# Chunked attention and a gated MLP on one core: v tiles used twice, keys put in place by two copies, a new order of the first blocks

## The chip, the core and the metric

The kernel runs on one core of a Trainium2 chip. The metric is the device time of one execution in microseconds. The kernel before takes 733.04 us, the median of 3 runs (732.32 to 733.74). One further execution was recorded by the profiler; every row shown here is from it.

The core's engines each work through a list of their own and wait for one another by semaphores: TensorE (PE in the rows, its weight loads PEld) multiplies matrices, VectorE (DVE), ScalarE (ACT) and GpSimd (POOL) work elementwise, SyncE (SP) issues most DMAs. SBUF is the working memory of 128 partitions, PSUM the one that TensorE writes.

## What is computed

Attention over 4 batches, 8 heads, 768 positions of 64 numbers, in chunks of 32 queries. A chunk sees 8 memory rows, 16 positions to its left, its own 32 and 8 to its right. The result goes through a gated MLP with RMS norm:

```python
for c in range(nc):                                   # 24 chunks of 32
    k_ctx = k[:, :, max(0, 32*c - 16):min(S, 32*c + 40)]      # v_ctx alike
    k_full = np.concatenate([mem_k, k_ctx], axis=2)           # v_full alike
    a = softmax(q_c @ k_full.T / 8)
    out[:, :, 32*c:32*c + 32] = a @ v_full
x = out as (3072 tokens, 512)
xn = x / sqrt(mean(x * x) + 1e-6) * rms_g
return (silu(xn @ w_gate) * (xn @ w_val)) @ w_out     # 512 -> 1536 -> 512
```

## The kernel before

**Tiling.** Tokens are cut into 8 blocks of 384. A unit of attention is one pair of heads in one block, four units a block. Blocks 0 and 1 (units 0 to 7, the two halves of batch 0) are done first, beside the preparation of the weights; the other blocks' units are done later between the MLP's matmuls. Each weight is used as the sum of a high and a low part, so each product of the MLP is three passes (`PASS`): the group of twelve matmuls for one hidden group of 128 is `pg` (gate) or `pv` (up), the group of nine is `po` (output). The two parts are made in the kernel: a chunk of weights arrives by DMA, ScalarE makes two passes over it (`w_open`, lines 508 and 509), VectorE does bit operations (`w_clamp`, `w_sign`, `w_shift`), ScalarE rounds it (`w_high`), VectorE subtracts (`w_low`, line 532). Chunks come in threes, gate, up, output: the first three hold hidden group 0, the next three groups 1 and 2.

**An early unit.** q and k arrive with four positions in each partition. TensorE transposes them (`t` for q, `T` for k) into PSUM. `Q` copies q into a tile that holds the two heads on separate halves. `K`, `n`, `c` copy k into the tile `kw`, which has for each chunk a column group of 64: 8 memory keys, 16 left, 32 own, 8 right. `p` lets GpSimd write the memory columns of `kw`. `V` fills the unit's v tile `vw` with copies of the memory rows and of the column of ones (for the softmax's sum), and `w` loads the v rows into it, 56 rows for each pair of chunks. Then: scores `S`, maximum `M`, subtraction `a`, exponential `E`, transpose `P`, its two copies `C` and `m`, the product with v `O`, and `X`, `x`, `u`, which divide by the sum. `A`, `B`, `D` transpose a finished block and split it into `xh` and `xl`.

**What sets the order.** Up to the middle of the MLP of blocks 0 and 1, the order on each engine is that of a string of tokens, `ORDER`: a letter from the list above and a unit or step, and at the end, where there is one, the engine that copies (a ScalarE, d VectorE, g GpSimd). The rest is ordered by a planner. `Z` loads the next weight chunk, `J F f I H L` are the six steps over it, `g v h i j k l o` the MLP (up to `g5`, `SEQ` tells which block and group), `W` runs matmuls on zeros. SyncE issues DMAs in the string's order as well; an issue waits for the eighth issue before it to land.

In the listing and the rows lines have the numbers of the kernel before. `finish` writes the last block.

Of the kernel before, what the change touches and what calls it, by code (L numbers as in the profile page):

```python
# [18 lines left out]
NM = 8  # L19
# [28 lines left out]
U0 U1 U2 V1a U3 V2a V3d V0g Z p1 T0 Q0a p0 t1 n0d c0a p3 w0 K0a Q1a S0 p2 T1 M0 p4 w1 a0 t2 c1a  # L48
K1a n1d e0 T2 Q2a S1 E0 n2d K2d c2a Z J P0 M1 p5 w2 t3 C0a f m0a S2 a1 Q3a T3 p6 M2 E1 U4 a2 P1 w3
O0 n3d m1a F C1a K3d V4g c3a O1 E2 X0 I U5 S3 x0 V5g J X1 u0 U6 P2 x1 M3 p7 W8 C2a Z f m2a w5 a3  # L50
Ha O2 u1 E3 L V6g P3 X2 t4 F m3a U7 x2 C3a I T4 Q4a w6 u2 O3 K4d c4a N0 n4d V7g X3 S4 x3 w4 u3 t5
M4 Ha a4 T5 Q5a L T6 c5a n5d Y0 K5d Z K6d t6 w7 n6d c6a y0 E4 S5 Q6a P4 M5 r0 S6 z0 C4a m4a W4 a5
J M6 t7 E5 f T7 a6 Q7a F P5 n7d K7d m5a A0 c7a I C5a S7 B0a Ha A1 M7 W5 B1a D0 E6 a7 Z A2 J D1 A3
L O4 B2a f W9 X4 E7 D2 B3a x4 P6 F W6 C6a D3 m6a u4 O5 Z J I O6 X5 f P7 g0 Ha X6 x5 x6 u5 C7a m7a
u6 v0 h0 F N1 L Z I O7 J X7 i0 Ha x7 g1 j0 u7 k0a L Y1 l0 v1 y1 f Z h1 r1 z1 o0 J i1 F j1 A12 A11
I B12a A13 B11a g2 D12 k1a Ha l1 Z D11 B13a A10 L v2 B10a h2 D10 J i2 o1 D13 f j2 g3 J F f k2a l2
v3 I h3 i3 Z Ha o2 f j3 F g4 k3a L l3 I v4 h4 i4 J Z F g5 Ha f j4 I o3 L Ha v5 k4a F Z J l4 L h5
o4 i5 I g6 j5 Ha f k5a l5 v6 J Z L h6 f o5 i6 F j6 g7 F k6a l6 I J o6 f Z h7 v7 F Ha i7 I g8 j7 Ha
I k7a l7 Ha v8 Z L h8 i8 J o7 L j8 L g9 k8a l8 F Z J o8 f h9 f v9 F i9 I g10 J j9 Z f k9a Ha F v10
l9 I h10 i10 o9 Ha I Z j10 Ha L g11 k10a l10 J L o10 h11 F i11 Z J f v11 L f I F g12 Ha j11 I k11a  # L60
Z J l11 v12 f Ha F L h12 i12 o11 L j12 Z J I g13 f k12a F Ha I v13 L Ha l12 L h13 Z J o12 i13 f
j13 F g14 k13a I l13 Ha L Z J o13 f h14 F I v14 i14 Ha L g15 j14 Z J k14a f l14 F v15 h15 I i15 Ha
g16 j15 J L f F o14 I Ha L v16 k15a l15 h16 o15 i16 j16
# [4 lines left out]
def tile_kernel(ctx: ExitStack, tc: tile.TileContext, q, k, v, mem_k, mem_v,  # L68
# [49 lines left out]
    late_kv = {}  # L118
    KW, VW = (NC + 1) * KC, NJ * 2 * (D + 1)
# [54 lines left out]
    def stage_v(u, e="a"):  # L174
# [4 lines left out]
        d["v"] = vw = unit_tile(u, [P, NJ, 2, D + 1], "vw", NG)  # L179
# [73 lines left out]
    def stage_k0(u, e="d"):  # L253
        own = NM + LC
        k4 = split4(st[u]["tk"], HT + CH)
        copy(e, st[u]["kw"][:, :, own:own + CH].rearrange("p c (k r) -> p c k r", r=4), k4)

    def stage_l0(u, e="d"):
        z = units[u][1] + NC
        k4 = split4(st[u]["tk"], HT + CH)  # L260
        copy(e, st[u]["kw"][:, 1:z, NM:NM + LC].rearrange("p c (k r) -> p c k r", r=4), k4[:, 0:z - 1, (CH - LC) // 4:])

    def stage_c0(u, e="a"):
        a = units[u][1]
        k4 = split4(st[u]["tk"], HT + CH)
        copy(e, st[u]["kw"][:, a:NC, KC - RC:KC].rearrange("p c (k r) -> p c k r", r=4), k4[:, a + 1:NC + 1, 0:RC // 4])
# [345 lines left out]
    def finish(f, g, vv, po, blk):  # L612
# [10 lines left out]
        for i in range(NT):  # L623
# [168 lines left out]
    def tok_o(n):  # L792
# [9 lines left out]
        T=stage_kt, t=stage_qt, K=stage_k0, n=stage_l0, c=stage_c0, p=new_kw, Q=stage_q0,  # L802
# [126 lines left out]
```

## Time and profile before

| | |
|---|---|
| median of 3 timed runs | 733.04 us |
| profiled execution | 731.54 us |
| its span in the trace | 729.8 us |
| TensorE, VectorE, ScalarE, GpSimd busy | 715.1, 380.0, 287.8, 36.4 us |
| mean granted clock of TensorE | 0.995 of full |
| bytes moved | 50.20 MB |

The span is the time from the first to the last recorded instruction; the execution's own time is 1.7 us more. A row of the timeline has the start in us, the length in us, engine, line, operation, what is written and from what, the shape and the count; at its end in brackets the idle time before it and what ended that. A row of groups has busy us and the mean in ns of one, and behind the second bar the idle time before these instructions. In the chain of waits each piece is what the next piece waited for.

### The profile page before, as it was taken

To read this page: it belongs to the slowest core of one execution; us is meant where nothing else is said; L and a number is where in the kernel's file an instruction comes from. 1 tells how busy PE (TensorE), PEld (TensorE's weight loads), DVE (VectorE), ACT (ScalarE), POOL (GpSimd) and SP (SyncE) were. 2 spreads that over 40 slices of the span, in tenths; PEclk is the share of its full clock that TensorE was granted. 3 is DMA by queue.
4 is the path that set the end of the run, shared out by engine and by line. 5 is a ranking of instruction groups with operands and counts; after the bars stand their busy time and mean duration, and the time that the engine had idled before them with its cause. 6 is when DMAs were issued, how large, how long until landed. Compare 5 with 4: busy or idle time off the path is not lost.

```text
span 729.8 us, 13052 instructions
## 1 busy us (share of the span) xinstructions
PE 715.1 (98%) x5136; PEld 656.6 (90%) x5136; DVE 380.0 (52%) x725; ACT 287.8 (39%) x600; POOL 36.4 (5%) x143
## 2 busy tenths in 40 slices
PE   8889999999999999999999999999999999999997
PEld 7778999999989999899999999989998999999996
DVE  4888999865645443444535353445434543332222
ACT  4899676643452323422333232432234222341112
POOL 3300000001000000000000000000000000000000
PEclk8999999999999999999999999999999999999999
DMA  8994563414412320122212123021311210010001
GB/s 173 203 259 141 173 202 116 132 37 102 85 37 68 55 50 22 62 46 42 43 38 66 23 45 61 20 66 31 66 29 34 64 32 20 20 44 0 1 1 43
DMA packets 143173, 50.20 MB, mean 69 GB/s; under 512 B 126984, under 2 KB 134536, under 8 KB 143112
## 3 DMA queue, kind: packets, MB, share of 16 engines
q1 hardware_dynamic: 139832, 44.49, 26.6%
q10 hardware_dynamic: 3280, 4.88, 1.8%
q8 instruction: 40, 0.66, 0.4%
q14 instruction: 21, 0.17, 0.1%
HBM read 43.06 MB, written 6.29 MB: 68 GB/s over the span
## 4 chain that ended last, share of the span: by engine, by line
PE 92%; ACT 3%; DMA 3%; DVE 1%; issue 0%; POOL 0%; ACTq 0%; SPq 0%; POOLq 0%
PE pv L561 28%; PE po L599 28%; PE pg L561 27%; PE s L318 3%; PE o L368 3%; PE xT L440 1%; PE pT L348 1%; DMA ws<-in_moe_w_val_dram 1%; DMA memV<-in_mem_v_dram 1%; DMA vw<-in_v_dram 1%; ACT junk L398 0%; ACT ws L508 0%; ACT pt L227 0%; DMA kv<-in_v_dram 0%; ACT qb L227 0%
## 5 line engine op out<-in xcount | busy, mean ns | idle before, releaser
L561 PE MATMUL pv<-xh,wh_v 128*128 128x384 f32 x384 | 132.8, 346 | 0.0
L561 PE MATMUL pg<-xh,wh_g 128*128 128x384 f32 x384 | 129.7, 338 | 0.7 <-DVE t L572 0.7
L561 PE MATMUL pv<-xh,wl_v 128*128 128x384 f32 x384 | 129.5, 337 | 0.6 <-DVE wl_v L532 0.6
L561 PE MATMUL pg<-xh,wl_g 128*128 128x384 f32 x384 | 129.5, 337 | 0.0
L561 PE MATMUL pg<-xl,wh_g 128*128 128x384 f32 x384 | 129.3, 337 | 0.0
L561 PE MATMUL pv<-xl,wh_v 128*128 128x384 f32 x384 | 129.3, 337 | 0.0
L572 DVE SCALAR_TENSOR_TENSOR t<-t,pg 128x384 f32<-128x384 f32 x96 | 53.1, 553 | 138.6 <-ACT t L568 138.5
L227 ACT CAST hh<-t 128x384 fp32r<-128x384 f32 x95 | 48.7, 512 | 174.9 <-PE po L599 165.3
L599 PE MATMUL po<-wh_o,hh 128*128 128x512 f32 x285 | 113.8, 399 | 0.3
L599 PE MATMUL po<-wh_o,hl 128*128 128x512 f32 x285 | 113.1, 397 | 0.0
L599 PE MATMUL po<-wl_o,hh 128*128 128x512 f32 x285 | 112.1, 393 | 0.0
L584 DVE TENSOR_TENSOR hl<-t,hh 128x384 fp32r<-128x384 f32 x95 | 52.9, 557 | 100.7 <-ACT hh L227 95.7
L568 ACT ACTIVATE t<-pg 128x384 f32<-128x384 f32 x96 | 47.2, 492 | 135.9 <-PE pg L561 130.8
L575 DVE TENSOR_TENSOR t<-t,pv 128x384 f32<-128x384 f32 x95 | 52.5, 552 | 64.9 <-PE pv L561 64.4
L561 PEld LDWEIGHTS pg<-xh,wh_g 128*128 128x128 f32 x384 | 72.1, 188 | 4.4 <-DVE t L572 0.9
L561 PEld LDWEIGHTS pg<-xl,wh_g 128*128 128x128 f32 x384 | 72.1, 188 | 3.6
L561 PEld LDWEIGHTS pv<-xh,wh_v 128*128 128x128 f32 x384 | 72.1, 188 | 2.4
L561 PEld LDWEIGHTS pv<-xh,wl_v 128*128 128x128 f32 x384 | 72.2, 188 | 0.9 <-DVE wl_v L532 0.9
L561 PEld LDWEIGHTS pv<-xl,wh_v 128*128 128x128 f32 x384 | 72.2, 188 | 0.3
L561 PEld LDWEIGHTS pg<-xh,wl_g 128*128 128x128 f32 x384 | 72.1, 188 | 0.0
L599 PEld LDWEIGHTS po<-wh_o,hl 128*128 128x128 f32 x285 | 53.5, 188 | 14.1 <-DVE hl L584 1.8
L599 PEld LDWEIGHTS po<-wh_o,hh 128*128 128x128 f32 x285 | 53.5, 188 | 10.0 <-ACT hh L227 1.7
(112 smaller groups left out, 772.9 us busy)
## 6 DMA issues: line engine op xcount, KB each, us to landing
kn<-in_k_dram SPq DMA_DIRECT2D x96, 52.0 KB
qn<-in_q_dram SPq DMA_DIRECT2D x96, 48.0 KB
out_dram<-ob ACTq DMA_DIRECT2D x18, 256.0 KB
ws<-in_moe_w_gate_dram SPq DMA_DIRECT2D x4, 1024.0 KB
ws<-in_moe_w_val_dram SPq DMA_DIRECT2D x4, 1024.0 KB
ws<-in_moe_w_out_dram SPq DMA_DIRECT2D x4, 1024.0 KB
kv<-in_v_dram SPq DMA_DIRECT2D x48, 84.0 KB
kv<-in_v_dram SPq DMA_DIRECT2D x48, 70.0 KB
```

Of the source, the lines that this page charges most:

```text
L227: return nc.scalar.copy(out, in_)
L318: on_pe(nc.tensor.matmul(s[64 * par:64 * par + 64, o:o + KC], lhsT=qb[:, c].rearrange("p s q -> p (s q)"), rhs=kw[:, c], start=True, stop= ...
L348: on_pe(nc.tensor.transpose(out=t[:, i * P:(i + 1) * P], in_=pe[:, i * P:(i + 1) * P], identity=ident))
L368: on_pe(nc.tensor.matmul(o[64 * par:64 * par + 64, c0:c0 + D + 1], lhsT=pt[:, i, 2 * par + hh].rearrange("p c q -> p (c q)"), rhs=d["v"][: ...
L440: on_pe(nc.tensor.transpose(out=t[:, i * P:(i + 1) * P], in_=tiles[i][:, kt * P:(kt + 1) * P], identity=ident))
L561: on_pe(nc.tensor.matmul(ps[:, 0:HT], lhsT=weight(a, n, f, kt), rhs=xs[c][:, kt], start=cnt == 0, stop=cnt == 3 * NKT - 1))
L568: nc.scalar.activation(t, g, AF.Tanh, scale=0.5)
L572: nc.vector.scalar_tensor_tensor(out=t, in0=t, scalar=1.0, in1=g, op0=ALU.add, op1=ALU.mult)
L575: nc.vector.tensor_tensor(out=t, in0=t, in1=vv, op=ALU.mult)
L584: nc.vector.tensor_tensor(out=hl, in0=t, in1=hh.bitcast(F32), op=ALU.subtract)
L599: on_pe(nc.tensor.matmul(po[i], lhsT=h[a][:, i * P:(i + 1) * P], rhs=weight(c, "o", f), start=f == 0 and n == 0, stop=f == NF - 1 and n == 2))
```

## The change

The v tiles of units 4 to 7 are those of units 0 to 3, with their memory rows still in place; GpSimd clears the 32 last rows of the last chunk pair (behind the end of the sequence) and writes the column of ones of the other half. A unit's keys are put in place by two copies: `K` writes left, own and right columns of eleven chunks at once (616 columns, ScalarE), reading overlapping windows; `n` writes the columns of the chunk at the open end (40 or 48, VectorE). `c` is gone. The last half of the last rows has a tile of its own and is stored by ScalarE's queue. The string is written anew.

```diff
 ORDER = """
-U0 U1 U2 V1a U3 V2a V3d V0g Z p1 T0 Q0a p0 t1 n0d c0a p3 w0 K0a Q1a S0 p2 T1 M0 p4 w1 a0 t2 c1a
+U0 U1 U2 U3 V0d p1 V1d Z V2d V3d T0 Q0a p0 w2 t1 n0d K0a p3 p2 Q1d S0 w0 T1 M0 a0 t2 K1a n1d e0
...
     def stage_v(u, e="a"):
...
-        d["v"] = vw = unit_tile(u, [P, NJ, 2, D + 1], "vw", NG)
+        if NG <= u < NE:
+
+            d["v"] = vw = first_v[u - NG]
+            nc.gpsimd.memset(vw[96:P, NJ - 1, :, 0:D], 0.0)
+            nc.gpsimd.tensor_copy(out=vw[:, :, :, D], in_=ones[hf])
+            return
+        d["v"] = vw = first_v[u] = unit_tile(u, [P, NJ, 2, D + 1], "vw", NG)
...
     def stage_k0(u, e="d"):
-        own = NM + LC
-        k4 = split4(st[u]["tk"], HT + CH)
-        copy(e, st[u]["kw"][:, :, own:own + CH].rearrange("p c (k r) -> p c k r", r=4), k4)
+
+        t = st[u]["tk"]
+        n = (HT + CH) // 4
+        src = bass.AP(t.tensor, t.offset + (CH - LC) // 4, [t.ap[0], [CH // 4, NC - 1], [1, (KC - NM) // 4], [n, 4]])
+        copy(e, st[u]["kw"][:, 1:NC, NM:KC].rearrange("p c (k r) -> p c k r", r=4), src)
 
     def stage_l0(u, e="d"):
-        z = units[u][1] + NC
-        k4 = split4(st[u]["tk"], HT + CH)
-        copy(e, st[u]["kw"][:, 1:z, NM:NM + LC].rearrange("p c (k r) -> p c k r", r=4), k4[:, 0:z - 1, (CH - LC) // 4:])
-
-    def stage_c0(u, e="a"):
-        a = units[u][1]
-        k4 = split4(st[u]["tk"], HT + CH)
-        copy(e, st[u]["kw"][:, a:NC, KC - RC:KC].rearrange("p c (k r) -> p c k r", r=4), k4[:, a + 1:NC + 1, 0:RC // 4])
+
+        hf = units[u][1]
+        k4 = st[u]["tk"][:, 0:HT + CH].rearrange("p (r k) -> p k r", r=4)
+        a, z = ((NM, KC - RC) if hf else (NM + LC, KC))
+        k0 = (NC * CH - LC) // 4 if hf else 0
+        copy(e, st[u]["kw"][:, NC * hf, a:z].rearrange("p (k r) -> p k r", r=4), k4[:, k0:k0 + (z - a) // 4])
...
             nc.scalar.activation(o[:, a], po[i][:, a], AF.Copy, scale=0.5)
-            nc.vector.tensor_scalar(out=o[:, b], in0=po[i][:, b], scalar1=0.5, scalar2=None, op0=ALU.mult)
+            ob = p1.tile([P, HT], F32, name="ob", tag="t")[:, 0:DM // 2]
+            nc.vector.tensor_scalar(out=ob, in0=po[i][:, b], scalar1=0.5, scalar2=None, op0=ALU.mult)
             nc.sync.dma_start(out=out[rows, a], in_=o[:, a])
-            nc.sync.dma_start(out=out[rows, b], in_=o[:, b])
+            nc.scalar.dma_start(out=out[rows, b], in_=ob)
```

What this makes of the lists is shown at three places; numbers behind the names tell tiles apart. The first is SyncE's list, where the second set of weight chunks is loaded (gate 128x4x512, up, output) beside unit 7's q and k (`qf`, `kf`) and the second half's v tiles (`vw`, five transfers each). Before:

```order
L156 DMA qf_560<-in_q_dram 96x2x256
L156 DMA kf_562<-in_k_dram 104x2x256
L211 DMA vw_540<-in_v_dram 56x6x64 x2
L205 DMA vw_540<-in_v_dram 48x2x64
L211 DMA vw_540<-in_v_dram 56x5x64 x2
L211 DMA vw_441<-in_v_dram 56x6x64 x2
L205 DMA vw_441<-in_v_dram 48x2x64
L211 DMA vw_441<-in_v_dram 56x5x64 x2
L496 DMA ws_672<-in_moe_w_gate_dram 128x4x512
L211 DMA vw_605<-in_v_dram 56x6x64 x2
L205 DMA vw_605<-in_v_dram 48x2x64
L211 DMA vw_605<-in_v_dram 56x5x64 x2
```

(one more v tile stands ahead of these rows, the chunks of up and output behind them), and after:

```order
L499 DMA ws_512<-in_moe_w_out_dram 128x1024
L157 DMA qf_517<-in_q_dram 96x2x256
L157 DMA kf_519<-in_k_dram 104x2x256
L503 DMA ws_619<-in_moe_w_gate_dram 128x4x512
L157 DMA qf_626<-in_q_dram 96x2x256
L157 DMA kf_628<-in_k_dram 104x2x256
L218 DMA vw_210<-in_v_dram 56x6x64 x2
L212 DMA vw_210<-in_v_dram 48x2x64
L218 DMA vw_210<-in_v_dram 56x5x64 x2
```

The gate chunk moved ahead of unit 7's q and k and of all four v tiles; up stands behind the second v tile, output behind the fourth.

The second is ScalarE's list where it makes the two passes over the up chunk (`ws_815` before, `ws_708` after) and later rounds it to `wh_v_89`. Before:

```order
L445 ACTIVATE xh_193<-xT_825,rg 128x384
L227 COPY pt_108<-pT_860 64x12x32 x2
L508 ACTIVATE ws_815<-ws_815 128x1024
L509 ACTIVATE wy_891<-ws_815 128x1024
L227 CAST wh_g_87<-wy_821 128x1024
L227 COPY pt_109<-pT_911 64x12x32 x2
L568 ACTIVATE t<-pg 128x384
L398 ACTIVATE junk,ss<-x 128x384 x3
L508 ACTIVATE ws_889<-ws_889 128x1024
L509 ACTIVATE wy_975<-ws_889 128x1024
L227 CAST wh_v_89<-wy_891 128x1024
```

After:

```order
L452 ACTIVATE xh_193<-xT_828,rg 128x384
L515 ACTIVATE ws_708<-ws_708 128x1024
L516 ACTIVATE wy_843<-ws_708 128x1024
L348 ACTIVATE pe_753<-pe_753 128x384
L348 ACTIVATE pe_820<-pe_820 128x384
L234 COPY pt_108<-pT_878 64x12x32 x2
L515 ACTIVATE ws_812<-ws_812 128x1024
L516 ACTIVATE wy_906<-ws_812 128x1024
L575 ACTIVATE t<-pg 128x384
L234 COPY pt_109<-pT_927 64x12x32 x2
L234 CAST wh_v_89<-wy_843 128x1024
```

The rounding of the gate chunk (`wh_g_87`) moved ahead of this piece, the sums of squares (`junk`) behind it, and two exponentials into it. On TensorE the groups g0, v0, g1, v1 keep their places, with unit 6's product and unit 7's transpose now between g0 and v0 (ahead of g0 before).

The third is VectorE's start, from the memory keys on. Before:

```order
L682 COPY memT<-pm 64x4x4x8 x2
L230 COPY vw_216<-memV 128x12x64
L230 COPY kw_239<-kT_228 128x11x16
L330 TENSOR_REDUCE mx_292<-s_266 128x6
L336 TENSOR_TENSOR pe_302<-s_266,mx_292 128x384
```

After:

```order
L690 COPY memT<-pm 64x4x4x8 x2
L237 COPY vw_210<-memV 128x12x64
L237 COPY vw_217<-memV 128x12x64
L237 COPY vw_222<-memV 128x12x64
L237 COPY vw_225<-memV 128x12x64
L237 COPY kw_239<-kT_228 128x40
L237 COPY qb_107<-qT_248 64x12x32 x2
L337 TENSOR_REDUCE mx_296<-s_269 128x6
L343 TENSOR_TENSOR pe_298<-s_269,mx_296 128x384
```

All four first v tiles get their memory rows from VectorE (one before, two from ScalarE and one from GpSimd), and unit 1's q copies (`qb_107`) came to it from ScalarE.

## Rows read from the trace of the kernel before

**Rows 1.** the page: busy time and instructions; TensorE in 40 slices (tenths busy).

```profile
PE 715.1 (98%) x5136; PEld 656.6 (90%) x5136; DVE 380.0 (52%) x725; ACT 287.8 (39%) x600; POOL 36.4 (5%) x143
...
PE   8889999999999999999999999999999999999997
```

**Rows 2.** stages: length, busy PE, PEld, DVE, ACT, POOL (count), clock, DMA share, GB/s.

```profile
13.00:20.00 7.00, 7.00 (x64) 6.12 (x64) 3.25 (x7) 4.75 (x11) 0.58 (x3) 0.52 0.89 184
20.00:36.00 16.00, 13.83 (x254) 12.23 (x251) 14.04 (x34) 12.82 (x36) 5.67 (x13) 1.00 1.09 194
36.00:50.00 14.00, 11.49 (x183) 9.48 (x178) 11.19 (x23) 12.79 (x25) 0.61 (x1) 1.00 0.99 253
50.00:61.00 11.00, 9.78 (x114) 8.96 (x111) 9.57 (x19) 10.72 (x22) 0.00 (x0) 1.00 0.72 233
```

**Rows 3.** chain of waits, 40 to 64 us: start, length, what ended last.

```profile
42.63 7.62 DMA ws<-in_moe_w_val_dram
...
50.28 1.23 ACT ws L508
...
52.43 1.07 ACT wh_g L227
...
59.83 1.24 DVE wl_v L532
...
61.10 2.02 PE pv L561 x10
```

**Rows 4.** SyncE's DMA issues: start, length, operation.

```profile
39.59 0.39 SPq L496 DMA_DIRECT2D ws<-in_moe_w_gate_dram  x1
```

**Rows 5.** ScalarE by shape, 8 to 61 us: busy, mean ns | idle before.

```profile
L227 ACT COPY qb<-qT 64x384 f32<-64x384 f32 x16 | 7.6, 473 | 1.2 <-PE qT L240 1.1
L341 ACT ACTIVATE pe<-pe 128x384 f32<-128x384 f32 x8 | 4.2, 523 | 0.1
L227 ACT COPY vw<-memV 128x768 f32<-128x768 f32 x2 | 1.6, 830 | 3.3 <-DMA memV<-in_mem_v_dram 3.3
L227 ACT COPY kw<-kT 128x416 f32<-128x416 f32 x2 | 1.0, 512 | 0.0
L227 ACT COPY kw<-kT 128x96 f32<-128x96 f32 x4 | 1.0, 239 | 2.1 <-PE kT L240 1.1 <-DVE kw L230 0.8
L227 ACT COPY kw<-kT 128x88 f32<-128x88 f32 x4 | 0.9, 233 | 1.1 <-DVE sr L411 0.6 <-DVE kw L230 0.5
```

**Rows 6.** VectorE's groups by shape, same stretch.

```profile
L230 DVE COPY kw<-kT 128x416 f32<-128x416 f32 x6 | 3.4, 581 | 0.0
L230 DVE COPY kw<-kT 128x176 f32<-128x176 f32 x4 | 1.4, 339 | 2.2 <-PE kT L240 1.7 <-ACT kw L227 0.5
```

**Rows 7.** timeline, GpSimd beside VectorE, then VectorE alone.

```profile
22.73 0.82 POOL L229 COPY vw<-memV 128x768 f32<-128x768 f32 x1 [1.59 <-DMA vw<-in_v_dram]
...
22.84 1.26 DVE L524 SCALAR_TENSOR_TENSOR wy<-wy,ws 128x512 uint32<-128x512 uint32 x1
...
28.46 0.69 DVE L524 SCALAR_TENSOR_TENSOR wy<-wy,ws 128x512 uint32<-128x512 uint32 x1
```

**Rows 8.** timeline, the first memory copy on VectorE and the first scores.

```profile
8.15 0.56 DVE L230 COPY vw<-memV 128x768 f32<-128x768 f32 x1 [0.19 <-DMA memV<-in_mem_v_dram]
...
11.31 0.88 PE L318 MATMUL s<-kw,qb 128*64 128x64 f32 x23 [2.45 <-POOL kw L221]
```

**Rows 9.** timeline, last xh, a transpose of three, a product of twelve.

```profile
48.18 0.58 ACT L445 ACTIVATE xh<-xT,rg 128x384 fp32r<-128x384 f32 x1
...
48.67 0.52 PE L348 MATMUL pT<-ident,pe 128*128 128x128 f32 x3 [1.26 <-DVE r L386]
...
56.15 0.92 PE L368 MATMUL o<-vw,pt 128*64 128x65 f32 x24
```

**Rows 10.** chain of waits, 60 to 70 us: one group of twelve.

```profile
66.20 2.11 PE pg L561 x12
```

**Rows 11.** timeline, VectorE's half of the last rows.

```profile
726.43 0.42 DVE L636 TENSOR_SCALAR ob<-po 128x256 f32<-128x256 f32 x1 [2.14 <-ACT ob L635]
```

More of the change, by code (lines that the diff above doesn't have):

```diff
@@ L47 @@
 ORDER = """
-U0 U1 U2 V1a U3 V2a V3d V0g Z p1 T0 Q0a p0 t1 n0d c0a p3 w0 K0a Q1a S0 p2 T1 M0 p4 w1 a0 t2 c1a
[L49 to L63, printed above, removed]
+U0 U1 U2 U3 V0d p1 V1d Z V2d V3d T0 Q0a p0 w2 t1 n0d K0a p3 p2 Q1d S0 w0 T1 M0 a0 t2 K1a n1d e0
@@ new lines @@
+E0 w1 T2 Q2d p4 S1 K2a n2d P0 J M1 p5 Z t3 m0a U4 a1 C0a S2 Q3d E1 w3 T3 p6 M2 F P1 K3a n3d a2 U5
+O0 C1a f m1a S3 X0 E2 I P2 p7 M3 Ha O1 x0 m2a V4 a3 C2a W3 u0 V5 E3 X1 O2 L Z J U6 x1 f P3 V6 C3a
+u1 t4 m3a X2 F x2 T4 I Q4a u2 O3 K4a n4d Ha S4 V7 X3 x3 N0 L t5 u3 M4 W9 Z Q5d J U7 a4 w4 Y0 F T5
+f t6 n5d K5a I w5 E4 Q6d T6 Ha S5 n6d K6a y0 L J P4 Z M5 w6 S6 z0 m4a r0 W9 M6 C4a a5 w7 a6 t7 f
+E5 T7 Q7a F P5 K7a n7d A0 I m5a S7 C5a B0a A1 M7 Ha Z W5 D0 a7 B1a A2 L A3 B2a W8 B3a D1 J D2 O4
+E6 D3 O5 X4 f P6 E7 g0 X5 C6a x4 x5 m6a u4 Z J F u5 O6 h0 I P7 v0 X6 m7a i0 C7a x6 f Ha O7 u6 L g1
@@ new lines @@
+N1 Z X7 j0 x7 k0d J v1 u7 F Y1 l0 I o0 h1 y1 i1 Z f Ha g2 r1 z1 J j1 A11 L A12 k1a A13 B11a v2 l1
+B13a D11 h2 D13 B12a i2 A10 o1 D12 B10a j2 J D10 F g3 k2a f l2 v3 I h3 i3 Z Ha f o2 L j3 g4 F k3a
+l3 I o3 h4 J F Z i4 Ha v4 f I g5 j4 Ha F k4d I v5 Z l4 Ha L o4 h5 i5 J L g6 j5 f k5a l5 Z J v6 F
+h6 f o5 i6 F j6 L g7 k6a l6 J I o6 h7 f Z Ha i7 v7 L F g8 j7 I k7a l7 Ha v8 Z I h8 J i8 L o7 Ha j8
+L g9 k8a l8 f Z J o8 F h9 f v9 i9 F I J g10 j9 Z f k9a Ha I v10 l9 Ha L h10 o9 i10 Z J F j10 L g11
+k10a l10 f o10 h11 I i11 Z J F Ha f v11 L F I g12 j11 Ha I k11a Z L J l11 Ha v12 f h12 F L o11 I
@@ L64 @@
+i12 Ha Z j12 J g13 L k12a f l12 F o12 h13 I i13 Ha Z J L v13 f F I g14 j13 Ha k13d L Z J l13 v14 f
+h14 F I o13 i14 Ha j14 L J Z g15 k14d f F l14 v15 I h15 i15 Ha L g16 J j15 f F o14 I Ha L v16 k15d
+l15 h16 i16 o15 j16
 """
@@ L118, in tile_kernel @@
     late_kv = {}
+    first_v = {}
     KW, VW = (NC + 1) * KC, NJ * 2 * (D + 1)
@@ L800, in tile_kernel @@
         U=tok_U, w=lambda n, *e: dma_v(n, *e), Z=lambda n: w_load(), W=warm,
-        T=stage_kt, t=stage_qt, K=stage_k0, n=stage_l0, c=stage_c0, p=new_kw, Q=stage_q0,
+        T=stage_kt, t=stage_qt, K=stage_k0, n=stage_l0, p=new_kw, Q=stage_q0,
         V=lambda n, e=None: stage_v(n, e or ("d" if n < NG else "a")),
```

## The prediction

> **What bounds the kernel now.** I read the page first: its busy shares and its 40 slices, where TensorE's row is to be looked at slice by slice [rows 1]. From the fourth slice on it is full; the first three, 55 us, are not. TensorE is busy for 715.1 us of 729.8, so a change of order can only win in the stretch before it fills. Everything behind that stretch is a fixed stream of matmuls and moves as a block.
>
> So the question is when the block starts, and the second view is the table by stage [rows 2]. Read the four stages across. From 13 to 20 us TensorE is busy for all 7 us, but at a granted clock of 0.52: nearly the whole stage stands at the lower of its two levels, 1.2 GHz. From 20 us on the clock is full, TensorE has gaps, and the two engines that copy are the busy ones: ScalarE 12.82 of 16, 12.79 of 14 and 10.72 of 11 us, VectorE 14.04, 11.19 and 9.57. The DMA share is near 1 up to 50 us.
>
> The third view, the chain of waits, says which of these ends last [rows 3]. The second weight chunk of the up projection (hidden groups 1 and 2; I call it val1, and its neighbours gate1 and out1) is in flight from 42.63 to 50.26 us. ScalarE takes it at 50.28, and from there it is ScalarE's list, one instruction behind the other, up to VectorE's subtraction at 59.83, which makes the low part of these weights; TensorE's matmuls on val1 (v1 from here on) start at 61.10. The start of v1 is my milestone: what it moves, the end moves by. In both programs the same products stand before it (all eight early units, then g0, v0, g1). SP issued gate1 at 39.59 us, behind three of the second half's v tiles [rows 4].
>
> The sum is made against the profiled execution (731.54 us, span 729.8), and its difference is then put on the 733.04 us median of the timed runs, 1.5 us more.
>
> **Transfers.** In SP's new order gate1 stands ahead of unit 7's q and k and of three v tiles (410 kB and 340 kB each, from the shapes in SP's rows, four bytes an element); val1 passes two v tiles. At 194 GB/s [rows 2] that is 1,430 kB, 7 us, for gate1, and at 253 GB/s 680 kB, 2.7 us, for val1. No byte is saved: what they pass lands that much later. Those v tiles are needed last by the products of units 6 and 7, behind g0. So val1 would land near 47.5 us instead of 50.26, and that is about when ScalarE reaches it (below).
>
> **ScalarE.** Removed: two copies of v's memory rows at 0.830 us, five pairs of q copies (ten at 0.473), eight right-context copies (four at 0.239, four at 0.233) and two key copies of 416 columns at 0.512: 9.3 us. Added: eight key copies of 616 columns; from 0.239 us at 96 and 0.512 at 416 columns, 0.853 ns each, one is 0.68 us, 5.5 together [rows 5]. Net -3.8 us. But nearly all of that falls on units 0 to 3, in the stage in which TensorE at half clock sets the pace. For units 4 to 7 it is 4 x 0.68 added against two q pairs (1.89) and four right-context copies (0.93): -0.1 us, nothing. What goes with the small copies there is the idle time before them, 1.1 us, in which they waited for VectorE [rows 5]. The two copies that put keys in place now wait for each other in the same manner, which may give some of it back.
>
> **VectorE.** Added: ten q copies of 384 columns (from 0.339 us at 176 and 0.581 at 416: 0.55 each, 5.5), three copies of v's memory rows at 0.56 (1.7), eight copies of 40 or 48 columns (about 0.2 each, 1.6). Removed: six copies at 0.581 and eight near 0.34, 6.3 us. Net +2.5 us [rows 6, 8]. Against it, four GpSimd copies of 768 columns go away. Beside one of them VectorE's 512-column bit operation took 1.26 us, alone 0.69 [rows 7]: 0.57 us for one, nothing to 2.3 for four; I take 1.1. So +1.4 us in all. About 4 us of the added work (three memory copies and three q pairs, less what goes) falls before 20 us, where VectorE is busy for only 3.25 of 7 us [rows 2]; behind that it has 2.6 us less to do than now. I cost it at nothing; what it costs without that cover is the third rival.
>
> **The first scores.** They start at 11.31 us now [rows 8]. Afterwards they need VectorE's four copies of memory rows from 8.15 us (4 x 0.56, to 10.4), its 40-column copy (0.2) and then ScalarE's 616 columns (0.68): 11.3, no change. GpSimd's nine small copies for the same tiles run at the same time, and the pair of rows that gave 0.57 us says that the two engines hinder each other [rows 7]. Bounds: 0.3 us earlier, if copies follow each other faster than their busy time, and 1.3 later, with the small copies one after another between VectorE's. I take 0. The Trainium skill, "SBUF — State Buffer", section "SBUF: two separate sides", has it as a lock: the two engines share a port pair, and whoever holds it makes the other wait out its whole instruction. The rows agree in direction, and by that rule the start would be taken at the later bound.
>
> **From val1 to v1.** ScalarE now has its last xh (the rounded x tile) done at 48.76 us [rows 9]. With equal work behind 23 us the new list has it there too if all waits stay, and about 2 us earlier, at 46.8, if ScalarE never waits from 26 us on. The 1.1 us of idle that goes puts it at 47.6, and the passes over val1 are next. From there the new order runs: the two passes, 2.15 us (50.28 to 52.43 [rows 3]); one exp, 0.52 [rows 5]; unit 6's transpose, 0.52 [rows 9]; then TensorE alone, back to back: g0, unit 6's product, unit 7's transpose, v0, unit 7's product, g1: three groups of twelve at 2.11 [rows 10], two products at 0.92, one transpose at 0.52 [rows 9], 8.7 us. Together 11.9 us: v1 at 59.5, with 58.7 and 60.7 as the ends. val1's low half does not bind: from its passes to VectorE's start it takes 9.55 us now, and even at that length, with the 1.24 of the subtraction [rows 3], it is ready at 58.4. v1 is 1.6 us earlier than 61.10, between 0.4 and 2.4.
>
> **The end.** VectorE takes the last half row block at 726.43, with its idle time before it ended by ScalarE's half [rows 11]; it still waits for ScalarE in the new program (both read one PSUM tile). I cost the other queue at 0, between -0.4 (VectorE's own 0.42, if it could start together with ScalarE's half) and the same length lost to a slower issue.
>
> **Sum.** -1.6 + 0 + 0 = -1.6 us on 733.04: 731.4 us. This measurement can tell about 0.2%, 1.5 us, from no change: the forecast lies at that line.
>
> **Rivals.** First, nothing to measure: ScalarE's waits stay and v1 starts at 60.7 (-0.4, 732.6), or the two engines' copies at the start hold each other up by the 1.3 us and eat most of the gain (-0.3, 732.7). This second way is the lock of the Trainium skill's page. For the rival: ScalarE's work behind 23 us is equal, and the new order puts a product and a transpose between g0 and v0. Against it: the chain names a transfer and small copies that both move away.
>
> Second, more: the first scores come 0.3 us early, ScalarE never waits (2.4), and the stage from 13 to 20 us keeps some of the full clock. At 0.52 it took 7 us; all at full it would be 3.6, of which VectorE's and ScalarE's lists might let 1 us through. -3.7 us, 729.3. Against it: TensorE is as idle before the first scores as now.
>
> Third, slower: VectorE becomes the bound at val1's low half. Its list ahead of it grows by the 1.4 us and by the first bit operation on out1, which the new order puts in front (1,024 columns, about 1.2 us by the 0.69 for 512). Its added q copies can only follow TensorE's transposes, at half clock; if they are not done in the idle time before 20 us and push the rest, v1 comes 2.6 us later, at 63.7, and the kernel takes 735.6. From 13 to 61 us VectorE has 10 us of idle [rows 2]; the case decides once less than 1 us of it is filled beyond what the first part of the list costs.
>
> **Chances.** The forecast 0.52 (0.32 of it beyond the line, 0.20 short of it); the first rival 0.20, of which 0.02 end as slower; the second 0.16; the third 0.12. Faster 0.48, same 0.38, slower 0.14. The forecast's own range is 730.6 to 732.6; with the rivals, until two tenths are left out, 729.2 to 734.4.
>
> **What would show it.** Right: gate1 issued before 36 us and val1 landed before ScalarE's passes over it, these near 47.6; v1 between 58.7 and 60.7; TensorE without waits behind it. A wait of TensorE for VectorE's low half of val1 is the third rival; first scores after 12.3 us are the held-up copies; a stage from 13 to 20 us at a clock well over 0.52 is the second rival. Wrong altogether: v1 earlier and the end not, through new waits of TensorE behind 61 us.

## The result and the profile after

The changed kernel takes **733.92 us** (median of 20 runs, 731.78 to 737.86), the kernel before, run beside it, **732.23 us** (20 runs, 730.72 to 734.96). The ratio is 1.0024, with a 95% interval of 1.0013 to 1.0036: 1.7 us slower, by 1.0 to 2.6. The forecast was 731.4 us, 1.6 us faster. The time lies outside the forecast's own range (730.6 to 732.6) and inside the wider one with its rivals (729.2 to 734.4), and it moved to the side that got a chance of 0.14.

The profiled execution took 733.74 us, with a span of 732.0. I read it in the order in which I read the one before. The page, busy time and TensorE's slices, against [rows 1]:

```profile
PE 717.5 (98%) x5140; PEld 658.8 (90%) x5140; DVE 383.2 (52%) x737; ACT 281.5 (38%) x581; POOL 33.7 (5%) x142
PE   8989999999999999999999999999999999999997
```

TensorE is busy for 2.4 us more, ScalarE for 6.3 less. The table by stage, the columns as in [rows 2]:

```profile
13.00:20.00 7.00, 7.00 (x56) 6.52 (x57) 3.70 (x8) 3.32 (x6) 0.79 (x4) 0.50 0.78 149
20.00:36.00 16.00, 14.28 (x256) 12.67 (x254) 13.77 (x35) 13.14 (x33) 2.98 (x12) 0.98 1.07 239
36.00:50.00 14.00, 11.76 (x182) 9.68 (x182) 12.40 (x24) 13.15 (x22) 1.25 (x1) 1.00 0.95 184
50.00:61.00 11.00, 9.55 (x119) 8.61 (x116) 8.14 (x17) 8.27 (x14) 0.00 (x0) 1.00 0.85 290
```

From 50 us on ScalarE, which was full before (10.72 of 11 us), is idle for 2.7 us, and v1 is no earlier for it. The chain of waits from gate1's transfer to v1, against [rows 3] (start, length, what):

```profile
26.82 11.92 DMA ws<-in_moe_w_gate_dram
...
38.77 1.17 ACT ws L515
...
45.04 0.94 PE s L325 x24
...
49.33 1.01 PE o L375 x27
50.34 0.78 issue
51.13 0.93 PE o L375 x21
52.06 0.48 PE pT L355 x3
52.53 2.10 PE pg L568 x12
...
58.06 0.67 issue
58.73 0.93 PE o L375 x24
59.66 2.29 PE pg L568 x12
61.94 2.10 PE pv L568 x12
```

ScalarE takes gate1 as it lands (38.77); eleven of the twelve profiles with the new order have a wait for it there, 0.07 us in this one. Its passes over val1 (48.75) are off the chain; they stand 9.98 us further down its list, and this distance is 9.9 to 10.2 us in ten of the twelve. So their start follows from the landing of gate1. Behind them TensorE stands twice where the forecast had it back to back, 0.78 and 0.67 us. What it stood for at 58.06 is in ScalarE's timeline:

```profile
52.57 0.96 ACT L234 COPY pt<-pT 64x384 f32<-64x384 f32 x2 [0.81 <-PE pT L355]
54.93 1.17 ACT L515 ACTIVATE ws<-ws 128x1024 int32<-128x1024 uint32 x1 [1.40 <-DMA ws<-in_moe_w_out_dram]
55.99 1.12 ACT L516 ACTIVATE wy<-ws 128x1024 f32<-128x1024 f32 x1
57.14 0.49 ACT L575 ACTIVATE t<-pg 128x384 f32<-128x384 f32 x1
57.66 0.97 ACT L234 COPY pt<-pT 64x384 f32<-64x384 f32 x2
```

Read the brackets: ScalarE stands 1.40 us for the transfer of out1, does its two passes, then the activation of g0, and only then copies unit 7's transposed weights (57.66 to 58.63), without which unit 7's product (58.73) cannot start. SP's timeline says why out1 is late (the three chunks, then out1's row in the kernel before), and SP's table of waits between 28 and 50 us (engine, line, what it waited for, us in total, times, longest) what held SP:

```profile
26.82 0.39 SPq L503 DMA_DIRECT2D ws<-in_moe_w_gate_dram  x1
41.55 0.39 SPq L503 DMA_DIRECT2D ws<-in_moe_w_val_dram  x1
48.75 1.23 SPq L499 DMA_DIRECT2D ws<-in_moe_w_out_dram  x1
```

```profile
43.52 1.42 SPq L492 DMA_DIRECT2D ws<-in_moe_w_out_dram  x1
```

```profile
SPq L218 <- DMA ws<-in_moe_w_gate_dram: 3.7, 1, 3.7
```

SP issues unit 5's first v load only when gate1, issued eight DMAs earlier, has landed (26.82 + 11.92 = 38.74). The v loads that are left stand behind it in SP's queue, ten of them between val1 and out1: 48.75, against 43.52 in the kernel before, where out1 follows val1 directly.

Of the 2.2 us between the two spans (729.8 and 732.0) two more parts lie elsewhere. The table shows when the first output product begins (behind v1), the steady stretch from the start of the third output product to the last matmul's end, and what follows that end; each is read from the timeline of the run's one profiled execution. "Wait" is TensorE's idle time right before unit 7's product.

| run | wait | first output product | steady | closing | median, us | ratio to before (95%) |
|---|---|---|---|---|---|---|
| before | - | 62.96 | 649.1 | 3.84 | 732.23 | |
| after | 0.67 | 63.88 | 649.3 | 4.66 | 733.92 | 1.0024 (1.0013 to 1.0036) |
| tail_old | 1.18 | 62.80 | 649.3 | 4.56 | 734.30 | 1.0020 (1.0006 to 1.0034) |
| tail_new | - | 63.31 | 649.1 | 3.84 | 732.77 | 0.9999 (0.9990 to 1.0008) |
| warm_after | 2.36 | 66.31 | 649.2 | 4.67 | 734.85 | 1.0028 (1.0018 to 1.0038) |
| warm_before | - | 64.09 | 648.9 | 3.84 | 732.42 | 0.9994 (0.9984 to 1.0004) |
| out1_later | 0 | 65.45 | 649.1 | 4.66 | 733.01 | 1.0001 (0.9988 to 1.0014) |
| out1_later_pad | 0 | 63.97 | 647.9 | 3.78 | 730.88 | 0.9981 (0.9966 to 0.9997) |
| reuse_only | - | 63.87 | 649.0 | 4.30 | 732.70 | 0.9990 (0.9977 to 1.0004) |
| keys_only | - | 63.63 | 648.9 | 3.83 | 732.54 | 1.0007 (0.9994 to 1.0021) |
| pads_only | 0.81 | 63.26 | 647.8 | 3.82 | 731.22 | 0.9980 (0.9966 to 0.9994) |
| out1_behind | 0 | 62.21 | 648.0 | 3.81 | 730.62 | 0.9969 (0.9955 to 0.9982) |
| u7_first | 0 | 67.14 | 648.0 | 3.80 | 733.79 | 1.0020 (1.0008 to 1.0033) |
| out1_sooner | 0 | 60.63 | 649.3 | 4.68 | 731.02 | 0.9985 (0.9969 to 1.0002) |
| addr_after | 0.98 | 61.52 | 647.8 | 4.66 | 732.65 | 1.0005 (0.9990 to 1.0019) |
| code_after | 2.32 | 64.82 | 649.1 | 3.79 | 732.74 | 1.0001 (0.9987 to 1.0016) |
| addr_before | - | 65.02 | 647.7 | 3.85 | 731.09 | 0.9976 (0.9963 to 0.9989) |
| sooner_pad | 0 | 60.29 | 648.1 | 3.78 | 729.35 | 0.9958 (0.9944 to 0.9972) |

In the two profiles, 0.9 us of the 2.2 are there by the first output product, 0.3 more by the third, 0.2 in the steady stretch, 0.8 behind the last matmul. The start of the first output product differs from one execution to the next: 62.80 and 63.88 with the same first 700 us, word for word; 61.52 to 64.82 in the five profiles that have the changed order up to there (after, tail_old, pads_only, addr_after, code_after), 62.96 to 65.02 in three that have that of before (before, tail_new, addr_before). So one profile cannot say what the order costs up to there. The medians of the runs, and the stretches inside the profiles, can.

### The profile page after: what moved, and what is told of

The parts are those of the page before. It is cut to its first block, busy times and chain, and to the rows that moved or that the text cites. A ratio compares the mean times of both kernels' runs of the same rounds, so it can differ in the third digit from the quotient of the medians.

```text
span 732.0 us, 13056 instructions
## 1 busy us (share of the span) xinstructions
PE 717.5 (98%) x5140; PEld 658.8 (90%) x5140; DVE 383.2 (52%) x737; ACT 281.5 (38%) x581; POOL 33.7 (5%) x142
## 4 chain that ended last, share of the span: by engine, by line
PE 95%; DMA 2%; ACT 1%; DVE 0%; POOL 0%; issue 0%; SPq 0%; POOLq 0%
PE pv L568 28%; PE po L606 27%; PE pg L568 27%; PE s L325 4%; PE o L375 3%; DMA ws<-in_moe_w_gate_dram 2%; PE xT L447 1%; PE pT L355 1%; PE pm L314 1%; DMA kv<-in_v_dram 0%; PE po L634 0%; PE qT L244 0%; PE kT L244 0%; PE warm L314 0%; PE qT L247 0%
## 5 line engine op out<-in xcount | busy, mean ns | idle before, releaser
L234 ACT CAST hh<-t 128x384 fp32r<-128x384 f32 x90 | 46.1, 512 | 170.8 <-PE po L606 160.6
```

The costliest lines, as they stand in the source:

```text
L234: return nc.scalar.copy(out, in_)
```

## The experiments

Each ran beside the kernel before on the same chip. The chip differs between groups of runs, so ratios are to be compared, not medians.

**tail_old: the old store in the new kernel; tail_new: the new store in the old one.**

```diff
-            ob = p1.tile([P, HT], F32, name="ob", tag="t")[:, 0:DM // 2]
-            nc.vector.tensor_scalar(out=ob, in0=po[i][:, b], ...)
-            nc.scalar.dma_start(out=out[rows, b], in_=ob)
+            nc.vector.tensor_scalar(out=o[:, b], in0=po[i][:, b], ...)
+            nc.sync.dma_start(out=out[rows, b], in_=o[:, b])
```

> The changed kernel with its last half row block stored as before: into one tile, from SP's queue. In the two profiles the last matmul ended 1.39 us later than before (725.99 and 727.38), but the span 2.2 us later: from the last matmul to the end it took 3.83 us before and 4.65 after. Theory A (ScalarE's queue is the dearer place for the last store): the stretch behind the last matmul falls back to about 3.8 us, the median from 733.9 to 733.1. Theory B (the end of a span varies from one execution to the next, and the queue has no part in it): it stays near 4.65, median 733.9. The first 700 us are those of the changed kernel word for word, so this run is also a second look at TensorE's clock at the start: if the 10.24 us at half clock come with the new order, they are here again and the third scores start near 20.75; if they are chance, they may be 6.83 us and the third scores near 19.5.

> The kernel before, with the last half row block in a tile of its own, stored from ScalarE's queue; nothing else changed. Theory A (the queue costs): from the last matmul to the end 4.65 us in place of 3.83, median 732.2 + 0.8 = 733.0. Theory B (it costs nothing): 732.2. Its start is the one of before: a second look at whether the half-clock stretch is 6.83 us there each time (third scores at 19.5).

Theory A fell twice: 4.56 us with the old store in the new kernel, 3.84 with the new store in the old one. The queue costs nothing; something else of the new program lengthens the end. And in tail_old the clock came back sooner, in the stage from 13 to 20 us:

```profile
13.00:20.00 7.00, 7.00 (x90) 6.50 (x89) 4.78 (x11) 4.29 (x8) 1.00 (x6) 0.80 0.82 149
```

0.80 granted in place of 0.50, with the same instructions: the time at half clock changes from one execution to the next. The third scores started at 18.19 (20.75 in the first profile), v1 at 60.71 (61.78).

**warm_after, warm_before: TensorE kept busy in the pause before the first scores.**

```diff
-p2 Q1d S0 w0        (after)        -K0a Q1a S0 p2        (before)
+p2 Q1d W28 S0 w0                   +K0a Q1a W34 S0 p2
```

> The changed kernel with 28 of the small matmuls on zeros put in front of unit 0's scores, where TensorE now stands idle for 2.0 us (9.2 to 11.2). They add no work to any other engine. Theory C (the time was lost to TensorE's clock, which falls to half behind this pause): the clock stays full from there on, the third scores start at about 18 us in place of 20.75, v1 near 60 in place of 61.8, and the median falls by 1.5 to 2.5 us to about 732. Theory D (ScalarE's and VectorE's lists and SP's transfers set the pace behind 22 us anyway, and clock only fills their waits): third scores as early, but v1 at 61.3 or later and the median at 733.5.

> The kernel before with 34 small matmuls on zeros in front of unit 0's scores, where TensorE stands idle for 2.45 us (8.9 to 11.3). Theory C (the clock sets the pace of the first blocks in both kernels): no stretch at half clock, third scores at about 17 in place of 19.5, v1 about 1.5 us before 61.1, median 730.5. Theory D (the lists set the pace): v1 at 61 and the median 732.

The granted clock was 1.00 over that stage in both, and the third scores of warm_after started at 17.37. It won nothing: ratios 1.0028 and 0.9994. Theory D holds. The third scores were 3.4 us earlier than in after, the passes over val1 only 0.25 (48.50). What the early start met, ScalarE's and TensorE's tables of waits of warm_after show (20 to 62 us and 50 to 66 us), and its clock from 60 to 63 us (columns as in [rows 2]):

```profile
ACT ws L515 <- DMA ws<-in_moe_w_out_dram: 6.0, 2, 3.2
```

```profile
PE o L375 <- issue: 2.4, 1, 2.4
```

```profile
60.00:63.00 3.00, 3.00 (x26) 2.88 (x22) 3.00 (x8) 2.53 (x8) 0.00 (x0) 0.50 0.08 32
```

Of the 6.0 us ScalarE stood 2.8 for the first output chunk, ahead of val1, and 3.15 for out1. The lead was waited off in front of transfers. But the clock did not stay full: it was at its lower level, 0.50, from 36.0 to 39.5 us and again from 59.9 to 63.3, behind TensorE's wait of 2.36 us, and g1 then took 3.28 us in place of the 2.19 of after. code_after has the same (a wait of 2.32, then 0.50, g1 in 3.62 us); behind the waits of 0.67 to 1.18 us in the other four profiles the clock stayed at 1.00. So a long wait for out1 is paid twice, and warm_after does not show what a clock that stays full would win with the new order. warm_before, whose granted clock is 1.00 over its whole profile, won nothing with the old one.

**out1_later: ScalarE's passes over out1 behind unit 7's copies.** J is the two passes, f VectorE's bit operation on them, Ha the rounding of val1, C7a unit 7's last copy.

```diff
-... x5 m6a u4 Z J F u5 ... i0 C7a x6 f Ha O7
+... x5 m6a u4 Z F u5 ... i0 C7a x6 Ha J f O7
```

> The changed kernel with one move: ScalarE's two passes over out1 (and VectorE's bit operation on them) stand behind unit 7's pT copies and behind the rounding of val1, no longer ahead of them. Theory A (ScalarE waits for out1's transfer with unit 7's copies queued behind it): in the three profiles of this program's start ScalarE stood 1.40, 1.94 and 3.15 us there, and TensorE then 0.67, 1.18 and 2.36 us before unit 7's product. Both waits go: at most 0.2 us before unit 7's product, v1 about 2.0 us after the end of v0 plus product and g1, that is 0.7 to 1.2 us earlier against the same stretch behind the start of g0 (g0 to v1 was 9.5 us in the changed kernel and 10.0 with the same start and a shorter half-clock stretch; 8.7 expected). Median 733.9 to about 732.9. Theory B (the wait only changes its place, the late out1 then holds up the first output product or g2): g0 to v1 as short, but TensorE waits behind v1 and the median stays at 733.9.

> The same move, and with it more instructions for GpSimd (8 small memsets near 66 us) and for SP (the three stores of one block are cut into four each), both far from the path, so that the last instructions of these two engines stand at other places in their code. In the changed kernel the closing sequence behind the last matmul takes 4.6 us in every profile, 3.84 in every profile of before's code, with the last store landed at 2.76 in all of them and whichever queue stores; the difference is two pauses of SP and GpSimd, 0.33 and 0.38 us, in which they wait for nobody. Theory A (they wait for code to be loaded, at a place that depends on how many instructions came before): both pauses go, 3.84 us, and the median is 0.7 us lower than that of the same move alone. Theory B (the pauses belong to the changed program's end in some other way): 4.6 us again.

The wait before unit 7's product went, but v1 did not come right behind g1. VectorE's and TensorE's waits from 50 to 66 us in out1_later:

```profile
DVE ws L525 <- ACT ws L515: 2.8, 1, 2.8
```

```profile
PE pv L568 <- DVE r L393: 1.4, 1, 1.4
```

VectorE now stood for ScalarE's pass, with the product on v0 behind it in its list (62.58 us), which frees v0's PSUM tile, and TensorE 1.4 us for that; the row names the reciprocal that starts as this product ends. The wait had moved. The ratio still went from 1.0024 to 1.0001. The second kernel also won the closing sequence, 3.78 us, as theory A said of it, but its steady stretch too was 1.2 us shorter, which neither theory had.

**reuse_only, keys_only: one part of the change in the order of before.** The first takes over the changed stage_v; the second the changed stage_k0 and stage_l0, with K on ScalarE and without the c tokens.

> The kernel before, in its own order, with the v tiles reused alone: units 4 to 7 take the tiles of units 0 to 3, clear 32 rows and set the ones, and three GpSimd copies and one ScalarE copy of v's memory rows go. Theory A (the reuse costs nothing and wins nothing by itself; the loss comes from the order of the transfers): v1 at 61.1 to 61.3, TensorE's end as before, median 732.2 to 732.7. Theory B (the reuse brings a new wait, its clearing copies stand behind the products and ahead of the loads of v): v1 after 62, median 733.5 or more. Theory C (GpSimd's big copies held VectorE up, and their removal helps): v1 at 60.5 or earlier.

> The kernel before with the keys put in place by two copies (ScalarE 616 columns, VectorE 40 or 48) for all eight units, the right-context copies dropped, all else in the order of before. Theory A (neutral): 5.5 us go to ScalarE and 2.9 leave it, VectorE is relieved; units 0 to 3 are hidden beside TensorE's transposes; ScalarE's list for units 4 to 7 grows by about 1.5 us, part of it hidden in its waits: v1 between 61.1 and 62.3, median 732.2 to 733.4. Theory B (the serial pair on one tile is slower than the three copies, which ran on two engines): S5 to S7 each later by 0.3 us and v1 past 62.3, median above 733.5.

The intervals of both contain no change. Neither the reuse nor the two copies is the cause by itself; what is left is the order, which was not run without them. The closing sequence of reuse_only, 4.30 us, is a third length, with before's store: SP pauses in it as in after (the traces hold 596 instructions of SP in both, 590 in before), GpSimd does not (206; 202 in after, 210 in before).

**pads_only, code_after, addr_after, addr_before: where the other 2 us of the padded kernels are from.** The pad is one unused column, eight GpSimd memsets, and one block's three stores cut in four; code_after has only the instructions, the addr kernels only the column.

```diff
+    pad = const.tile([P, 1], F32, name="pad")            # addr_*, pads_only
...
+        for _ in range(8):                               # code_after, pads_only
+            nc.gpsimd.memset(pad, 0.0)                   # code_after: zero[:, 0:1]
```

> The changed kernel in its own order with only the extra instructions for GpSimd and SP that shift the place of their last instructions in their code. Theory A (0.75 us of the loss is code that SP and GpSimd wait for in the closing sequence): 3.8 us behind the last matmul in place of 4.65, unit 7's product still behind a wait of 0.7 to 2.4 us, median 733.9 - 0.8 = 733.1, ratio to the kernel before about 1.001. Theory B (what the move of out1's passes won was the main part, the closing sequence little): ratio still 1.002 or more.

> The changed kernel with one column more in its constant pool, which nothing reads or writes; no instruction is added. It moves the place in SBUF of the tiles behind it. In the four kernels with the extra column and the extra instructions the stretch from the second output product (near 77 us) to the last matmul took 647.8 to 648.0 us, in the eight without them 648.9 to 649.3, with drifts that repeat with the hidden groups. Theory A (it is where the weights lie): 648.0 here too, the closing sequence still 4.6 us, ratio to the kernel before about 1.0008 in place of 1.0024. Theory B (it came with the extra instructions or the cut stores): 649.2.

> The changed kernel with the extra GpSimd memsets (on a column that is there already) and the three stores cut into four, but without the new column. Theory A (the place of the code decides the closing sequence, the place of the tiles the steady stretch): 3.8 us behind the last matmul, 649.2 us in the steady stretch, ratio about 1.0013. Theory B (both come from the instructions): 3.8 and 648.0, ratio 0.998.

> The kernel before with the same unused column. Theory A (the steady stretch depends on where the weights lie, whatever the change): 648.0 us from the second output product to the last matmul in place of 649.1, median 732.3 - 1.1 = 731.2, ratio 0.9985; so a part of what the kernels with the column win is no gain over the kernel before's order. Theory B (before's tiles lie well already, the loss of the steady stretch is the changed kernel's own): 649.1, ratio 1.000.

pads_only won more than its theory A said, and the next two divide it: the instructions give the closing sequence (3.79 us in place of 4.66, the steady stretch as it was), the column the steady stretch (647.8 in place of 649.3, the closing sequence as it was). The ratio fell by 0.0023 and 0.0019 with them, by 0.0044 with both. SP's wait for the other engines in the closing sequence, after, then code_after:

```profile
SPq L933 <- PEq L933: 0.9, 2, 0.5
```

```profile
SPq L938 <- PEq L938: 0.6, 2, 0.4
```

The longer wait is for GpSimd's pause; SP's own stands ahead of it. What they pause for stays open: in after the two pauses lie between 3.08 and 4.01 us behind the last matmul, and the trace has no packet of code in them; the first one there starts at 4.05.

The column works on the matmuls of the gate and of the up projection, not on those of the output (400, 397, 393 ns in after and 400, 397, 394 in addr_after). Line 568 or 569 from 100 to 700 us (count, busy us, mean ns), after and then addr_after:

```profile
L568 PE MATMUL pv<-xh,wh_v 128*128 128x384 f32 x340 | 117.9, 347 | 0.0
L568 PE MATMUL pg<-xh,wl_g 128*128 128x384 f32 x340 | 114.7, 337 | 0.0
```

```profile
L569 PE MATMUL pv<-xh,wh_v 128*128 128x384 f32 x344 | 118.8, 345 | 0.0
L569 PE MATMUL pg<-xh,wl_g 128*128 128x384 f32 x340 | 114.4, 336 | 0.0
```

addr_before has it as well (647.7 us, 0.9976), so it is no part of the change and none of its loss. Of code_after's profile one more pair of rows is worth reading, since there the trace names the link that it left as "issue" in after (ScalarE from 40 to 62 us, TensorE from 50 to 66):

```profile
ACT ws L515 <- DMA ws<-in_moe_w_out_dram: 3.1, 1, 3.1
```

```profile
PE o L375 <- ACT pt L234: 2.3, 1, 2.3
```

**out1_behind, u7_first: the passes further back; unit 7's q and k ahead of gate1.** Both have the pad.

```diff
-x6 Ha J f O7 ... k0d J v1          -W9 Z Q5d J U7        (u7_first only)
+x6 Ha O7 ... k0d J f J v1          +W9 U7 Z Q5d J
```

> The last kernel with the move and the extra instructions, and the passes over out1 moved further back, behind VectorE's product for the first hidden group (j0) and ScalarE's and VectorE's parts of it. In the run with the first move VectorE stood 2.8 us for ScalarE's first pass over out1, with the product that frees the PSUM tile of v0 queued behind it, and TensorE then 1.39 us before v1. Theory A (VectorE's wait is what holds v1 now): this wait goes, v1 starts right behind g1 or within 0.4 us, g0 to v1 8.7 to 9.2 us in place of 10.3, and the median falls by about 1 us, to 729.9. Theory B (the passes on out1 are then late for the first output product of the second weight chunk): TensorE waits before o1, near 71 us, by 1 us or more, and the median stays at 730.9.

> The same, with unit 7's q and k loaded ahead of gate1 and not behind it. In all profiles of the changed order TensorE stands 0.57 to 2.0 us at 41 to 42 us before unit 7's q is transposed, since it landed behind gate1 (39.1 to 41.3 us). Theory A (these waits are on the path): unit 7's scores start at 43.5 or earlier in place of 44.0 to 45.0, v1 0.5 to 1 us earlier, the median 729.4. Theory B (ScalarE's passes over gate1, which then land 1 us later, take the place): unit 7's scores at 44 to 45 as before, median unchanged against the run without it.

out1_behind: theory A on the wait; v1 starts 8.7 us behind g0 (51.42 to 60.13), and the first output product is 1.8 us earlier than in out1_later_pad. Of theory B's wait 0.6 us came, before g2. The median, 730.62, fell by 0.3 us between two chips, not by the expected 1; the intervals of the ratios, 0.9969 and 0.9981, overlap. u7_first: theory B, and dearer than it said. gate1 was in flight until 41.59, and ScalarE stood for it (20 to 62 us):

```profile
ACT ws L516 <- DMA ws<-in_moe_w_gate_dram: 4.5, 1, 4.5
```

**out1_sooner, sooner_pad: out1 loaded ahead of units 6's and 7's v.** Nothing else is moved; sooner_pad adds the pad.

```diff
-P4 Z M5 w6 ... Ha Z W5 D0
+P4 Z Z M5 w6 ... Ha W5 D0
```

> The changed kernel with its passes where it has them, but out1 loaded ahead of the v tiles of units 6 and 7 and not behind them. Theory A (what holds ScalarE up is the late transfer): out1 lands by 51 us in place of 54 to 56, ScalarE has no wait before its passes, unit 7's copies come in time and TensorE waits less than 0.3 us before unit 7's product; v1 0.7 to 1.2 us earlier after g0, median about 733. Theory B (the v tiles then come late instead): TensorE waits before the products of unit 6 or 7 by 0.7 us or more for a transfer, median 733.9.

> The changed kernel with out1 loaded ahead of the v tiles of units 6 and 7, and with the unused column and the extra instructions. Theory A (the three terms add up: 0.8 us in the closing sequence, 1.2 us in the steady stretch, and about 2 us in the first 75 us): v1 near 58.6 to 59.5, 648.0 us steady, 3.8 us at the end, median 729.0 to 729.5, ratio about 0.996. Theory B (the early out1 was only won by TensorE's clock, which stayed full in that one profile): v1 at 60.5 or later in this one, median 730.5.

Theory A both times, and the median of out1_sooner is 2 us below the 733 that it gave. ScalarE has no wait for out1 any more, and the chain of out1_sooner is the one that the prediction wrote down:

```profile
46.90 1.05 ACT ws L515
47.95 1.08 ACT wy L516
49.03 0.42 ACT pe L348
...
49.49 0.55 PE pT L355 x3
50.04 2.10 PE pg L568 x12
52.15 0.85 PE o L375 x24
52.99 0.48 PE pT L355 x3
53.47 2.10 PE pv L568 x12
55.58 0.85 PE o L375 x24
56.43 2.28 PE pg L568 x12
58.71 2.08 PE pv L568 x12
```

One load issued earlier turns 1.0024 into 0.9985, which is clear of the changed kernel but not of the kernel before; with the pad it is 0.9958, 729.35 us, faster than both. Since the pad's column gives 0.9976 to the kernel before as well, about 0.18% (0.9958 over 0.9976, 1.3 us) would be the order's own; the two intervals overlap, so six runs do not show it.

That the clock was full from the start in both of these profiles, so that their v1 may flatter, is theory B's point. One stretch does not depend on the start: from ScalarE's first pass over val1 to v1's first matmul, by the timeline. It takes 11.8 us in out1_sooner and in sooner_pad, and 13.0, 13.0, 15.7, 12.6, 15.6 and 12.8 in the six profiles with the wait (after, tail_old, warm_after, pads_only, code_after, addr_after), 13.8 on the mean. In after 0.5 of it belongs to the 0.78 inside unit 5's product. So the late out1 costs 0.7 to 4.0 us, 1.9 on the mean: the wait itself, and in two of them the lower clock behind it.

## Why the prediction was wrong

- **Transfers, and the path from val1 to v1: here it failed.** gate1 was issued before 36 us and val1 was there in time, as forecast. But the step ended at "what they pass lands that much later", and followed that delay only to the products of units 6 and 7. The third transfer in the same queue, out1, was not looked at: it went from 43.52 to 48.75, and the new order had put ScalarE's passes over it in front of unit 7's copies. So TensorE was not "alone, back to back" from g0 to v1: it stood 0.67 us before unit 7's product, 0.8 to 2.4 in the five other profiles. The prediction named the bit operation on out1 as work on VectorE's list (third rival), not as a wait for a transfer on ScalarE's.
- **ScalarE.** The passes over val1 began at 48.75, inside 46.8 to 48.8, but at its late end; 47.6 was taken. The six profiles with this order of loads and passes (those with the wait) have 46.6 to 48.8, 47.9 on the mean: the size was right. The reason was not: no idle time before small copies sets it, but gate1, which was issued 12.8 us earlier (26.82; the sum had 7), was in flight for 11.92 us, and has ScalarE begin at its landing.
- **From val1 to v1.** 11.9 us by the sum, 13.2 in the chain (48.75 to 61.94). 0.67 is the wait above; 0.78 stands inside unit 5's product, released by nothing that the profile shows. Of the five others only pads_only has it, with 0.23. It costs 0.5: unit 6's transpose starts 3.24 us behind the passes, 2.7 in the others. Its cause is left open. Without the waits the sum is right: 46.90 to 58.71 is 11.8 us in out1_sooner, and v1 at 58.7 is inside the forecast 58.7 to 60.7.
- **The milestone.** v1 did not start at 61.10 in the kernel before. Its first two matmuls, which need no low part of the weights, ran at 60.00 and 60.17; [rows 3] show the other ten. They took 2.02 us, a whole group takes 2.10, so the misreading costs the sum 0.1 us.
- **First scores.** 11.21 us, 0 as taken. GpSimd's copies were held up beside VectorE's, and only the first three:

```profile
8.39 0.66 POOL L225 COPY kw<-memT 128x96 f32<-128x96 f32 x1 [5.30 <-DVE memT L690]
8.99 0.51 POOL L227 COPY kw<-memT 128x8 f32<-128x8 f32 x1
9.44 0.53 POOL L228 COPY kw<-memT 128x8 f32<-128x8 f32 x1
...
10.64 0.26 POOL L225 COPY kw<-memT 128x96 f32<-128x96 f32 x1
10.84 0.19 POOL L227 COPY kw<-memT 128x8 f32<-128x8 f32 x1
```

  The first three ran while VectorE copied v's memory rows from SBUF to SBUF (8.36 to 10.39 us). The last two of these rows ran while it copied k and q out of PSUM (10.42 to 11.64), and took the 0.26 and 0.19 us that such copies take in the kernel before with VectorE idle. So 0.3 to 0.4 us were added to each of three, less than one VectorE copy of 0.56 [rows 8]. The lock of the Trainium skill's "SBUF — State Buffer", section "SBUF: two separate sides", agrees in direction. The later bound that the prediction gave to that rule (1.3 us) did not come: most of GpSimd's copies ran when VectorE's from SBUF were over, and VectorE's four took 2.03 us, no more than 4 x 0.56.
- **The end.** 0 for the queue was right (tail_new: 0.9999). The 0.8 us of the closing sequence was in no term; [rows 11] end at the last copy, and the stretch behind it was taken as fixed.
- **A block behind v1.** Nearly: +0.3 us up to the third output product (g2 waited 0.2, its transposes stand elsewhere; four of the six profiles have it) and +0.2 in the steady stretch, near 200 us. Neither was in the sum.
- **Rivals.** The second, with more of the full clock from 13 to 20 us, is not borne out: the clock was full there in warm_after and warm_before, and nothing was won. The third did not come true as written, since TensorE never waited for val1's low half; in the repair out1_later VectorE's list did become the bound, through a wait for ScalarE. The slower case that happened, an early load that makes a later one late, was on no list.

In sum, in the one profile v1 came 2.4 us later than forecast: 1.15 from passes that began late in this execution, 1.3 from the two waits behind them. Over the six profiles the passes began about where the forecast had them, and the late out1 cost 1.9 us on the mean, more than the 1.6 that were to be won. In the medians, 1.7 us were lost; +0.5 behind v1 and +0.8 at the end, both missing in the sum, leave about +0.4 up to v1, where -1.6 was forecast. With out1 loaded earlier (out1_sooner) the median is 1.1 us below before's although the +0.8 at the end is still in it: the gain that the forecast had.

## What to carry to other kernels

When a load is moved ahead in a queue, follow every load behind it to the instruction that waits for it, and what stands behind that instruction, not only the ones that it passes directly. On a list that runs in order, a pass over data in flight belongs behind the work that is ready. Differences of 0.2% need a look at things that no schedule shows: where the tiles and the last instructions lie.

## What the runs showed of the hardware

- One unused column of four bytes a partition in the constant pool shortened the gate and up projections' matmuls from 337 to 336 and from 347 to 345 ns on the mean; the steady stretch became 1.2 to 1.5 us shorter, in both kernels. Which address it is that matters was not tried.
- The closing sequence takes 4.6 to 4.7 us in the six kernels with 596 or 598 SP and 202 GpSimd instructions in their traces, 4.30 with 596 and 206, and 3.8 in the eleven others. Instructions added far from the end bring 4.66 to 3.79 us (code_after). Why SP and GpSimd pause is not shown.
- A GpSimd copy of 0.26 or 0.19 us took 0.66 and 0.51 to 0.53 beside VectorE's copies from SBUF to SBUF, and its usual time beside VectorE's copies out of PSUM.
- Behind TensorE's waits of 2.36 and 2.32 us before unit 7's product (warm_after, code_after) the granted clock fell to 0.50, and the next group of twelve took 3.28 and 3.62 us in place of 2.19; behind the waits of 0.67 to 1.18 us in the four other profiles it stayed 1.00.
- TensorE's granted clock from 13 to 20 us was 0.50 and 0.80 in two executions of the same first 700 us.
